# A second fold of the tokens ahead of a Fourier mixing step: fewer matmul columns for a longer chain of small operations

## The chip, the cores and the metric

One core of one Trainium2 chip. The metric is the device time of one execution in microseconds. The engines are named as the profile names them: PE is TensorE's matmuls, PEld its weight loads, DVE is VectorE, ACT is ScalarE, POOL is GpSimd. All data are fp32; each fp32 matmul shows in the trace as two records (the transform's 14 matmuls a batch as 28: 112 of `pz` and `pzt` in the four batches of the kernel before).

## The reference, cut to what matters

An mLSTM attention block produces `x` of 4 batches x 768 tokens x 320 features. Then comes a Fourier mixing and a two-layer MLP (1280 wide):

```python
def _moe_ref(x, w_ch1, w_ch2):
    X = np.fft.fft(x, axis=1)          # over the 768 tokens
    X = np.fft.fft(X, axis=2)          # over the 320 features
    u = x + np.real(X).astype(np.float32)
    ...                                # un = layer norm of u
    ch = np.maximum(un @ w_ch1, 0.0) @ w_ch2
    return (u + ch).astype(np.float32)
```

The transform over the tokens is a product with a table of cosines and sines, on TensorE.

## The kernel before: the parts that the change touches

The program is a schedule of small pieces (`at(slot, phase, piece, ...)`), interleaved so that the attention of batch n+1 and the MLP of batch n fill TensorE between the steps of the mixing. The code counts batches from 0, the text from 1, so `b == 0` is batch 1.

The mixing already uses one symmetry of the tokens, t with S - t: VectorE adds and subtracts paired row blocks (`eo`), then folds the 320 features in the same way into `fe`, so three row blocks of 128 tokens (`TG = 3`) are left instead of six.

```python
def mix_fold(b, p):
    ...
    for i, op in ((0, OP.add), (1, OP.subtract)):
        nc.vector.tensor_tensor(out=eo[:, i], in0=x[:, c], in1=x[:, m], op=op)
    ...
    ends(nc.vector, fe[:, p], 0, every)
    halves(nc.vector, fe[:, p, 1:HALF_D], 0, every, OP.add)
    halves(nc.vector, fe[:, p, PAD:PAD + HALF_D - 1], 1, every, OP.subtract)
    if p == TG - 1:
        nc.gpsimd.tensor_copy(out=fe_odd[:, 0:NC], in_=fe[:, p, 0:NC])
        ends(nc.gpsimd, fe_odd, 1, first)
        halves(nc.gpsimd, fe_odd[first, 1:HALF_D], 1, first, OP.add)

def mix_products(p, out, i, m):        # i = 0: cosine part, i = 1: sine part
    fm = slice(i * PAD + m.start, i * PAD + m.stop)
    kw = dict(stop=(p == 0), skip_group_check=True)
    if i == 0 and p == TG - 1:         # this block: even and odd frequencies apart
        nc.tensor.matmul(out[:, 0:NK:2], fe[:, p, fm], ds_sb[:, p, 0, 0:NE], start=True, **kw)
        nc.tensor.matmul(out[:, 1:NK:2], fe_odd[:, m], ds_sb[:, p, 0, NE:], start=False, **kw)
    else:                              # NK = 385 frequencies at once
        nc.tensor.matmul(out, fe[:, p, fm], ds_sb[:, p, i], start=(p == TG - 1), **kw)
```

`mix_seq` runs these products for features 0 to 127 (the two "big parts", cosine and sine, each into its own bank), `mix_tail` for the features left over: the cosine half of the tail writes partitions 0 to 63 of one bank, the sine half partitions 64 to 127 (a bank is a buffer into which TensorE writes results). For batches 2 to 4 the schedule gives each big part a slot of its own, with products of the MLP between:

```python
def plan_mix(b, s0, x_done, s_feat, s_add, s_turn):
    for j in range(TG):
        p = TG - 1 - j
        at(x_done[j], FILL + 0.5, mix_fold, b, p)
        if b == 0:
            ...
        else:
            at(s0, FILL_PE + 4, mix_seq, b, p, (0,))
            at(s0 + 1, FILL_PE + 4, mix_seq, b, p, (1,))
            at(s0 + 2, FILL_PE + 4, mix_tail, b, p)
```

In the MLP, VectorE's `add` (h = h + bank) frees the bank that a later product needs:

```python
    def add(h, bank):
        nc.vector.tensor_tensor(out=h, in0=h, in1=bank, op=OP.add)
```

## Time and profile before

| | before |
|---|---|
| time, first 3 runs | 446.88 us median (446.79 to 449.14) |
| profiled run: span, mean granted clock | 444.9 us, 0.996 |
| TensorE busy | 426.2 us, 96% |
| VectorE, ScalarE, GpSimd busy | 56%, 37%, 36% |
| the three changed transforms begin at | 142.91, 236.33 and 334.73 us |

TensorE, busy 96% of the span, is read here as the bound: a microsecond in which it stands still is counted as a microsecond lost. Two views that the prediction below uses in words only. The clock row of the page has one digit per fortieth of the span, 9 meaning 90% or more of full speed; the 8 is the half clock at the start-up (0.50 from 25.74 to 29.15 us):

```profile
PEclk9989999999999999999999999999999999999999
```

And TensorE's timeline at batch 2's tail (start, duration, operation, output<-inputs, count). Records of the cosine half (L627, L628) and of the sine half (L630) start together, at 156.28. The tail ends where the next group starts, at 158.37, so it takes 2.09 us:

```profile
156.28 0.35 PE L627 MATMUL pzt<-ds_sb,fe 128*64 128x193 f32 x1
156.28 0.54 PE L630 MATMUL pzt<-ds_sb,fe 128*64 128x385 f32 x1
...
156.95 1.49 PE L630 MATMUL pzt<-ds_sb,fe 128*64 128x385 f32 x8
158.37 1.88 PE L875 MATMUL po<-w_sb,hT 128*128 128x320 f32 x6
```

### The profile page before, as it was taken

Reading aid. Unit: us, or ns where it says so; the run is one execution under the profiler, and the core shown is the slowest. Engines: PE = TensorE matmul, PEld = TensorE weight load, DVE = VectorE, ACT = ScalarE, POOL = GpSimd, SP = SyncE. Lnnn points to the kernel's source line nnn. Section 1 sums busy time; section 2 is a strip of 40 time slices with the busy share of each in tenths; the row PEclk is TensorE's granted clock in tenths of the full one; section 3 lists DMA queues with packets and bytes.
Section 4 is the critical chain, followed back from the end, with each engine's and each line's share of the span. In section 5 each row is a group of like instructions: output and inputs, shape, how many; then the busy total and the mean of one; then the engine's idle time right before and its main releaser. Section 6 shows DMA issues by size and latency. Waiting matters only on the chain.

```text
span 444.9 us, 7313 instructions
## 1 busy us (share of the span) xinstructions
PE 426.2 (96%) x2680; PEld 285.4 (64%) x2680; DVE 250.5 (56%) x626; ACT 166.6 (37%) x442; POOL 159.0 (36%) x177
## 2 busy tenths in 40 slices
PE   8978989999899999989999999999999999999996
PEld 7767546666567777845556777775556677545774
DVE  8788784779986346587732266567630452343000
ACT  6957266584551223453243224443320031232000
POOL 5563101454333312045664303525661000477100
PEclk9989999999999999999999999999999999999999
DMA  7889944569364234157101432410000000000000
GB/s 238 257 237 338 285 129 134 184 195 288 110 177 138 76 123 137 55 156 219 40 1 49 139 119 97 125 31 1 2 0 15 16 26 18 16 0 1 31 29 29
DMA packets 20707, 47.37 MB, mean 106 GB/s; under 512 B 2816, under 2 KB 9344, under 8 KB 20544
## 3 DMA queue, kind: packets, MB, share of 16 engines
q1 hardware_dynamic: 20672, 46.91, 33.7%
q8 instruction: 21, 0.34, 0.3%
q14 instruction: 14, 0.11, 0.1%
HBM read 42.79 MB, written 4.11 MB: 105 GB/s over the span
## 4 chain that ended last, share of the span: by engine, by line
PE 75%; DVE 14%; issue 4%; ACT 3%; DMA 2%; POOL 2%; SPq 0%; DVEq 0%; POOLq 0%; ACTq 0%
PE po L875 29%; PE pm L822 13%; PE ps L455 4%; PE ph L476 4%; PE pm L827 4%; PE pu L661 4%; PE ph L469 3%; PE pz L630 3%; PE pm L760 3%; PE put L701 2%; PE pzt L630 2%; PE px L525 1%; DVE W L461 1%; DVE eo L588 1%; DMA G_d<-g 1%
## 5 line engine op out<-in xcount | busy, mean ns | idle before, releaser
L875 PE MATMUL po<-w_sb,hT 128*128 128x320 f32 x480 | 135.2, 434 | 0.0
L875 PEld LDWEIGHTS po<-w_sb,hT 128*128 128x128 f32 x480 | 89.7, 190 | 38.1 <-issue 2.0
L834 POOL TENSOR_SCALAR hT<-hT 128x384 f32<-128x384 f32 x45 | 66.2, 1492 | 86.2 <-DVE hT L831 86.2
L831 DVE TENSOR_TENSOR hT<-hT,pm 128x384 f32<-128x384 f32 x60 | 30.6, 549 | 38.2 <-ACT hT L853 25.7
L881 DVE SCALAR_TENSOR_TENSOR ot<-po,rstd,u 128x320 f32<-128x320 f32 x24 | 13.2, 548 | 69.0 <-PE po L875 69.0
L433 POOL TENSOR_SCALAR_AFFINE_SELECT W<-W 128x1024 f32<-128x1024 f32 x18 | 20.9, 1164 | 82.6 <-ACT W L411 78.6
L411 ACT ACTIVATE W<-W,colT 128x128 f32<-128x128 f32 x144 | 45.1, 395 | 0.0
L461 DVE TENSOR_TENSOR W<-ps,W 128x512 f32<-128x512 f32 x48 | 30.7, 680 | 10.7 <-POOL W L433 9.9
L822 PE MATMUL pm<-uT,w_sb 128*128 128x384 f32 x90 | 33.1, 496 | 1.6 <-DVE hT L831 0.9
L760 PE MATMUL pm<-uT,w_sb 128*128 128x384 f32 x80 | 29.6, 499 | 0.5 <-DVE u L683 0.4
L706 ACT COPY uT<-put 128x384 f32<-128x384 f32 x24 | 10.9, 480 | 49.6 <-PE put L701 49.6
L455 PE MATMUL ps<-qk 40*128 40x128 f32 x384 | 29.1, 290 | 0.2
L421 POOL TENSOR_TENSOR qg<-qk,Gb 128x512 f32<-128x512 f32 x19 | 26.4, 1388 | 4.9 <-DMA Gb<-G_d 4.8
L455 PEld LDWEIGHTS ps<-qk 40*128 40x128 f32 x384 | 24.5, 193 | 5.0 <-issue 1.0
L476 PE MATMUL ph<-W,kvt 128*41 128x128 f32 x384 | 26.2, 277 | 0.6 <-DVE W L461 0.6
L469 PEld LDWEIGHTS ph<-qg,C 128*128 128x128 f32 x160 | 20.8, 197 | 9.2 <-issue 3.2
L469 PE MATMUL ph<-qg,C 128*128 128x128 f32 x160 | 22.6, 286 | 3.9 <-POOL qg L421 2.4
L827 PE MATMUL pm<-uT,w1t_sb 64*128 64x384 f32 x120 | 25.2, 514 | 1.1 <-DVE hT L831 1.1
L822 PEld LDWEIGHTS pm<-uT,w_sb 128*128 128x128 f32 x90 | 16.1, 189 | 15.1 <-DVE hT L831 4.6
L476 PEld LDWEIGHTS ph<-W,kvt 128*41 128x41 f32 x384 | 19.7, 117 | 3.9 <-DVE W L461 1.0
L514 ACT COPY h<-ph 41x512 f32<-41x512 f32 (+1 forms) x16 | 9.3, 581 | 32.3 <-PE ph L476 32.2
L827 PEld LDWEIGHTS pm<-uT,w1t_sb 64*128 64x128 f32 x120 | 11.8, 185 | 12.3 <-issue 8.2
(164 smaller groups left out, 636.6 us busy)
## 6 DMA issues: line engine op xcount, KB each, us to landing
W<-M_d SPq DMA_DIRECT2D x18, 512.0 KB
kvt<-in_kv SPq DMA_DIRECT2D x24, 324.0 KB
qk<-in_qkT SPq DMA_DIRECT2D x48, 160.0 KB
raw<-in_w SPq DMA_DIRECT2D x10, 640.0 KB
Gb<-G_d SPq DMA_DIRECT2D x38, 128.0 KB
so<-in_o SPq DMA_DIRECT2D x24, 160.0 KB
out<-ot SPq DMA_DIRECT2D x24, 160.0 KB
ds_sb<-in_dft_s SPq DMA_DIRECT2D x1, 1155.0 KB
```

Of the source, the lines that this page charges most:

```text
L411: nc.scalar.activation(out=k.W[:, h, :], in_=M, func=AF.Exp, scale=-1.0, bias=colT[:, c, 0, b * H + h:b * H + h + 1])
L421: nc.gpsimd.tensor_tensor(out=k.qg, in0=k.qk[:, 0], in1=k.Gb, op=OP.mult)
L455: nc.tensor.matmul(k.ps[hip][:, p, :], k.qk[r, 1, p, :], k.qk[r, 0, p, :], start=True, stop=True)
L461: nc.vector.tensor_tensor(out=Wv, in0=k.ps[hip], in1=Wv, op=OP.mult)
L469: nc.tensor.matmul(k.ph[:, p, :], k.C[:, p, :], k.qg[:, p, :], start=(p == 0), stop=False, skip_group_check=True)
L476: nc.tensor.matmul(k.ph[hip * 64:hip * 64 + D1, p, :], k.v1[:, 2 * p + hip, :], k.W[:, 2 * p + hip, :], start=(c == 0 and p == 0), stop=Tr ...
L760: nc.tensor.matmul(k.pm[i], w1_sb[:, ch, f0:f0 + L], u[2 * ch], start=(ch == 0), stop=False)
L822: nc.tensor.matmul(bank, w, u, start=start, stop=True, skip_group_check=True)
L827: nc.tensor.matmul(bank, block(w1t_sb, i)[rows], mlp_u(gr, 1)[rows], start=False, stop=True, skip_group_check=True)
L831: nc.vector.tensor_tensor(out=h, in0=h, in1=bank, op=OP.add)
L834: nc.gpsimd.tensor_scalar(out=h, in0=h, scalar1=-1.0, scalar2=0.0, op0=OP.mult, op1=OP.max)
L875: nc.tensor.matmul(k.po, k.h[gr][f][:, i * L:(i + 1) * L], w2_sb[:, f, :], start=(f == 0), stop=(f == NFF - 1))
```

## The change

The intent: the 385 frequencies split into even and odd ones, and for each kind the table is symmetric or antisymmetric in t with S/2 - t. So blocks 0 (F) and 2 (F2) can be added and subtracted once more before the products. Each even or odd set then needs two row blocks in place of three: 3080 columns per batch instead of 4620, in the same number of matmuls (14). Table and output are then read and written with a stride of two. Batch 1 stays as it was. The core of the diff:

```diff
+    def mix_fold_again(b):
+        k = mixes.setdefault(b, Mix())
+        F, G, F2 = (fe[:, p] for p in range(TG))
+        k.less = eo_p.tile(...)  # cut
+        cos = (slice(0, 1), slice(0, NC))
+        nc.gpsimd.memset(F2[0:1, PAD:], 0.0)
+        nc.vector.tensor_tensor(out=k.less, in0=F, in1=F2, op=OP.subtract)           # L617
+        nc.gpsimd.tensor_copy(out=k.less[cos], in_=fe_odd[cos])                      # L618
+        nc.gpsimd.tensor_copy(out=fe_odd[:, 0:NC], in_=G[:, 0:NC])                   # L619
+        nc.gpsimd.tensor_tensor(out=fe_odd[cos], in0=G[cos], in1=F[cos], op=OP.subtract)  # L620
+        nc.gpsimd.tensor_tensor(out=G[cos], in0=G[cos], in1=F[cos], op=OP.add)       # L621
+        nc.vector.tensor_tensor(out=F, in0=F, in1=F2, op=OP.add)                     # L622
+        nc.gpsimd.tensor_copy(out=F[cos], in_=F2[cos])                               # L623
...
+    def mix_products_again(k, p, out, i, m):
+        ...  # F, G, less: the feature slices of the blocks
+        every, even, odd = slice(0, NK), slice(0, NK, 2), slice(1, NK, 2)
+        if i == 0:
+            products = ((even, F, 0), (even, G, 1), (odd, less, 0), (odd, fe_odd[:, m], 1))
+        else:
+            products = ((even, less, 0), (odd, F, 0), (every, G, 1))
+        for n, (cols, f, p) in enumerate(products):
+            nc.tensor.matmul(out[:, cols], f, ds_sb[:, p, i, cols], start=(n == 0), stop=(n == len(products) - 1),
+                             skip_group_check=True)
...
-            else:
+            elif j == 0:
+                at(x_done[-1], FILL + 0.55, mix_fold_again, b)
                 at(s0, FILL_PE + 4, mix_seq, b, p, (0,))
                 at(s0 + 1, FILL_PE + 4, mix_seq, b, p, (1,))
                 at(s0 + 2, FILL_PE + 4, mix_tail, b, p)
...
+    at(24, FILL + 0.4, lambda: nc.gpsimd.memset(ds_sb[0:1, 0, 0, :], 1.0))
```

The L numbers are the lines under which the changed kernel's profile shows them; its matmuls of the transform are L651, its MLP products L854 and L859, its MLP add L863. The one-row operations (`cos`) mend the first row of each block, whose tokens have no ordinary partner.

More of the change, by code (lines that the diff above doesn't have):

```diff
@@ L601, in mix_fold @@
         if p == TG - 1:
-            nc.gpsimd.tensor_copy(out=fe_odd[:, 0:NC], in_=fe[:, p, 0:NC])
+            if b == 0:
+                nc.gpsimd.tensor_copy(out=fe_odd[:, 0:NC], in_=fe[:, p, 0:NC])
             ends(nc.gpsimd, fe_odd, 1, first)
             halves(nc.gpsimd, fe_odd[first, 1:HALF_D], 1, first, OP.add)
+    def mix_fold_again(b):
+        k = mixes.setdefault(b, Mix())
+        F, G, F2 = (fe[:, p] for p in range(TG))
+        k.less = eo_p.tile([L, 2, DM], FP, name="eo", tag="eo").rearrange("p two n -> p (two n)")[:, 0:2 * PAD]
+        cos = (slice(0, 1), slice(0, NC))
[7 more added lines that the diff above has]
+        nc.gpsimd.tensor_copy(out=F[cos], in_=F2[cos])
     def mix_seq(b, p, parts):
@@ L612, in mix_seq @@
         for i in parts:
-            mix_products(p, k.pz[i], i, slice(0, L))
+            (mix_products if b == 0 else mix_products_again)(k, p, k.pz[i], i, slice(0, L))
     def mix_tail(b, p):
@@ L620, in mix_tail, with mix_products @@
         for i in range(2):
-            mix_products(p, k.pzt[i * 64:(i + 1) * 64], i, slice(L, PAD))
-    def mix_products(p, out, i, m):
+            (mix_products if b == 0 else mix_products_again)(k, p, k.pzt[i * 64:(i + 1) * 64], i, slice(L, PAD))
+    def mix_products_again(k, p, out, i, m):
+        fm = slice(i * PAD + m.start, i * PAD + m.stop)
+        F, G, less = fe[:, 0, fm], fe[:, 1, fm], k.less[:, fm]
+        every, even, odd = slice(0, NK), slice(0, NK, 2), slice(1, NK, 2)
[6 more added lines that the diff above has]
+                             skip_group_check=True)
+    def mix_products(k, p, out, i, m):
         fm = slice(i * PAD + m.start, i * PAD + m.stop)
```

## The prediction

> **What bounds the kernel now.** I read the busy table of the page first, then the slices and clock, then the chain of work that ended last, then the TensorE waits after 140 us, and last the timelines around each place where a batch's tokens are folded.
>
> ```profile
> span 444.9 us, 7313 instructions
> PE 426.2 (96%) x2680; PEld 285.4 (64%) x2680; DVE 250.5 (56%) x626; ACT 166.6 (37%) x442; POOL 159.0 (36%) x177
> ...
> PE 75%; DVE 14%; issue 4%; ACT 3%; DMA 2%; POOL 2%; SPq 0%; DVEq 0%; POOLq 0%; ACTq 0%
> ```
>
> TensorE is busy 96% of the span and carries 75% of the chain. So a microsecond of matmul saved is a microsecond saved, and a microsecond in which TensorE is made to wait is one lost. The waits of TensorE from 140 us to the end, where all three changed folds lie, add up to only 3.4 us:
>
> ```profile
> PE pm L827 <- DVE hT L831: 1.1, 1, 1.1
> PE pm L822 <- DVE hT L831: 0.9, 4, 0.3
> PE pm L822 <- DVE uT L810: 0.6, 1, 0.6
> PE pz L630 <- DVE fe L595: 0.5, 1, 0.5
> PE pm L822 <- DVE ot L881: 0.3, 1, 0.3
> ```
>
> Two places matter. Batch 2 has no slack between fold and transform: its transform starts at 142.91 and then waits for VectorE's last fold (timeline, TensorE and VectorE):
>
> ```profile
> 143.56 0.81 PE L630 MATMUL pz<-ds_sb,fe 128*128 128x385 f32 x2
> 144.91 0.91 PE L630 MATMUL pz<-ds_sb,fe 128*128 128x385 f32 x2 [0.54 <-DVE fe L595]
> ...
> 143.39 1.24 DVE L591 COPY fe<-eo 128x2 f32<-128x2 f32 x1
> 144.55 0.81 DVE L595 TENSOR_TENSOR fe<-eo 128x159 f32<-128x159 f32 x2
> ```
>
> Batches 3 and 4 fold at 216 and 315 us and transform at 236 and 335 us, 20 us later. But right after the fold VectorE's queue holds adds that free banks for the running MLP, and the chain runs through VectorE there:
>
> ```profile
> 215.64 0.55 DVE L595 TENSOR_TENSOR fe<-eo 128x159 f32<-128x159 f32 x2
> 216.10 0.54 DVE L831 TENSOR_TENSOR hT<-hT,pm 128x384 f32<-128x384 f32 x1
> ...
> 218.86 1.47 DVE L831 TENSOR_TENSOR hT<-hT,pm 128x384 f32<-128x384 f32 x3
> ```
>
> The second tail product of the MLP (started 216.84) needs the add that ended at 216.64: 0.2 us of slack. The next block, at 219.46, already waited 0.22 us.
>
> [...] after the idle around 22 to 25.5 us the granted clock was 0.50 from 25.7 to 29.1 us. That window still held 0.86 us of matmuls in 3.41[...]. [...] the two tail halves write partitions 0-63 and 64-127: both start at once, and the tail takes 2.1 us, not the 3.9 us of its records in series. [...] the stride-2 outputs of the first row block (193 columns) ran 0.163 us a record, just their columns, so I take no penalty. [...]
>
> **The change part by part.** Removed, for batches 2 to 4: matmul columns. Every fp32 matmul shows as two records; a record of 385 columns takes 0.323 us (six in 1.94), one of 193 takes 0.163. Before, the cosine and the sine part each took 1155 columns, 1.94 us. Now they are four times 193 (8 x 0.163 = 1.30) and 193+192+385 (1.30). The number of matmuls and weight loads stays 14; loads don't bind, because 128-column records elsewhere (eight in 0.89 us) sustain 0.11 us. Two big parts save 0.64 us each. The tail, if its halves still overlap, goes from 2.09 to about 1.44, saving 0.65. That is 1.94 us a batch, 5.8 us in all.
>
> Added: a chain that hops between VectorE and GpSimd. In order: subtract of 128x384 on VectorE, 0.56 (the 128x384 subtracts of the MLP's sums: 0.557); GpSimd copy 1x161, 0.35, and copy 128x161, 0.35 (348 ns, same instruction as the removed one); two GpSimd tensor-tensors of 1x161, 0.51 each (512 ns for 1x159); add of 128x384 on VectorE, 0.56, which must wait for the two because they read the row it overwrites; then a GpSimd copy 1x161, 0.35. Each hand-over costs 0.06 to 0.07 us, as between GpSimd's dependent casts. VectorE is held from its first to its last of these: 0.62 + 0.41 + 0.42 + 0.58 + 0.58 + 0.63 = 3.2 us. To the last copy it is 3.65 us. The 192-element memset (0.26 us, estimated from 120 ns for 31 and 525 ns for 512 elements) precedes it and is hidden. One memset of a table row at slot 24 is off the path.
>
> Where it lies. Batch 2: all products now need the complete second fold; the built order puts the first behind the last GpSimd copy. The ordinary fold should end about 145.2 [...], so TensorE restarts at about 148.9 and stands still for 6.0 us from 142.9. The group of output products that began at 145.82 begins at 148.9 + 1.3 = 150.2: 4.4 us late. The sine part gives back 0.64 and the tail 0.65: net 3.1 us lost. [...] Batch 2: +4.4.
>
> Batches 3 and 4: the built order has the subtract and the waiting add ahead of the MLP's add, so that add starts at 219.3 instead of 216.1, and everything of VectorE behind it (13 small operations, three adds) moves too. TensorE stops about 3.2 us less slack in each batch, roughly 3.1 to 3.2; later 1.94 come back: +1.25 each. The stop is about 2.4 us of true idleness[...]. Together +2.9.
>
> Sum: 446.9 + 4.4 + 2.9 = 454.2; I say 454.0, since a stop lets the other engines catch up and may swallow some of the 2 us that TensorE waits for VectorE at 190 to 197 us.
>
> **The rivals.** (a) The matmuls decide: if TensorE were not stopped, because the second fold hid in the 20 us of slack, the result would be 446.9 - 5.8 = 441. For it: 96% busy, and the real slack in batches 3 and 4. Against it: batch 2 has none, and the slack is of the transform, not of VectorE's queue[...]. (b) The halves of the tail don't overlap any more: program order now has four products (eight records) of one half before the other's first, where it had two; then the tail takes 2.6 us and the result is 3.4 us worse, 457.5. [...] I give it 20%. (c) The clock never halves: 452.5. Against it: the drop at 25.7 us. (d) Stride-2 reads of the table or more weight switches make a 193-column record as long as a 385-column one: all 5.8 us vanish, about 460. The table's old half was contiguous, so no line excludes it; I give it 7%.
>
> **Range and chances.** From 450.0 (no halved clock and part of the stops swallowed elsewhere) to 457.5 (serial tail or both clock drops). Slower by over 2% means above 455.8: 0.25. Faster by over 2%, below 437.9, would need more than the whole saving: 0.02. Within 2%: 0.73.
>
> **What would show it.** TensorE busy time falls in the transform: pz from 1.94 to 1.30 us a part, tail near 1.4. In batch 2 a TensorE wait near 6 us for GpSimd's last copy, with the clock at half shortly after. In batches 3 and 4, VectorE's add waits about 2 us for GpSimd, and a TensorE tail product waits 2.4 to 3 us for VectorE. Wrong if the waits of TensorE after 140 us stay near 3.4 us, if the records of 193 columns last over 0.2 us apiece, or if the chain passes through GpSimd's ReLUs instead.

How the sum came about: it was 446.9 + 4.4 + 2.9 = 454.2 us, given as 454.0. The 4.4 of batch 2 are the 3.1 above and 1.25 for a lower clock after the stop; the 2.9 are 1.25 and 0.2 for a lower clock in each of batches 3 and 4. These three terms, 1.65 us in all, were the estimate, and what they rested on was not shown by the trace before, which has one stretch of half clock in its span (25.74 to 29.15 us, after the window of 22.33 to 25.74 with 0.86 us of matmuls). The 145.2 us for the end of the ordinary fold and the 20% for rival (b) stand as estimates.

## The result, and the profile after

| | before | after |
|---|---|---|
| time, median of 6 runs | 448.09 us (446.79 to 450.89) | 463.88 us (462.70 to 465.35) |
| ratio of fast runs | | 1.0348 [1.0310, 1.0386] |
| profiled run: span, mean clock | 444.9 us, 0.996 | 463.6 us, 0.966 |

The ratios here and below are the mean time of one kernel's fast runs over that of the other's in the same rounds, so not quite the ratio of the medians. The change is slower by 3.5%, against 1.6% predicted; 463.88 lies above the range.

The page of the changed kernel, the same lines as shown of before:

```profile
span 463.6 us, 7339 instructions
PE 435.5 (94%) x2680; PEld 294.0 (63%) x2680; DVE 253.6 (55%) x632; ACT 166.6 (36%) x442; POOL 165.1 (36%) x193
...
PEclk9979999999999799997979999999989999999999
...
PE 80%; DVE 11%; ACT 3%; issue 2%; DMA 2%; POOL 2%; SPq 0%; DVEq 0%; POOLq 0%; ACTq 0%
```

TensorE has a third fewer transform columns in three batches and yet was busy 9.3 us longer. The clock row points to why: four further digits are below 9. A matmul at half clock counts as busy for about twice as long: the first four records of the transform took 1.45 us in batch 2 (150.83 to 152.28, clock 0.50) and 0.69 us in batch 3 (253.02 to 253.71, clock 1.00). The chain ends up in TensorE more than before (80% for 75%), not less.

The waits of TensorE from 100 us on (longest last):

```profile
PE pz L651 <- POOL fe L623: 5.6, 1, 5.6
PE pm L859 <- DVE hT L863: 5.4, 3, 2.2
```

The first is the one stop of batch 2; of the second line's three waits two are the new stops of batches 3 and 4, and the third, 1.1 us, was there before. Batch 2 in TensorE's timeline:

```profile
150.83 1.66 PE L651 MATMUL pz<-ds_sb,fe 128*128 128x193 f32 x4 [5.58 <-POOL fe L623]
152.28 0.85 PE L651 MATMUL pz<-ds_sb,eo 128*128 128x192 f32 x2
152.92 0.85 PE L651 MATMUL pz<-ds_sb,fe_odd 128*128 128x192 f32 x2
153.56 2.74 PE L907 MATMUL po<-w_sb,hT 128*128 128x320 f32 x6
```

From 150.83 to 153.56 are 2.73 us for eight records that the prediction put at 1.30. Batch 3, where the fold itself is needed only at 253.02, but VectorE's queue is held by it (first fence VectorE, second TensorE):

```profile
227.19 0.56 DVE L617 TENSOR_TENSOR eo<-fe 128x384 f32<-128x384 f32 x1
229.73 0.56 DVE L622 TENSOR_TENSOR fe<-fe 128x384 f32<-128x384 f32 x1 [1.98 <-POOL fe L621]
230.21 0.55 DVE L863 TENSOR_TENSOR hT<-hT,pm 128x384 f32<-128x384 f32 x1
```

```profile
230.81 2.93 PE L859 MATMUL pm<-uT,w1t_sb 64*128 64x384 f32 x6 [2.15 <-DVE hT L863]
```

VectorE waits 1.98 us for GpSimd's L621 in the middle of the fold, the MLP's add (L863) stands behind it, and TensorE waits 2.15 us for that add. Batch 4 has the same wait, 2.15 us at 335.22.

Now the clock. The windows view gives per stretch (us from the start) the busy time of PE, PEld, DVE, ACT and POOL with counts, then the mean granted clock of TensorE, the DMA share and GB/s. In this trace half clock begins at 25.79, 148.66, 206.69, 230.58 and 336.40 us, each time for 6.83 or 3.41 us, and at 462.69, to the end; all the changes lie whole multiples of 3.413 us apart. The stretches are cut there, to a tenth, and are called windows below. First batch 2's stop, then batch 3's, then batch 4's, each with what followed:

```profile
145.30:148.70 3.40, 0.00 (x0) 0.00 (x0) 2.47 (x5) 0.00 (x0) 2.27 (x4) 0.99 0.11 40
148.70:152.10 3.40, 1.27 (x4) 1.27 (x5) 2.22 (x4) 0.00 (x0) 2.51 (x6) 0.50 0.19 65
152.10:155.50 3.40, 3.40 (x10) 2.81 (x9) 1.13 (x2) 1.70 (x6) 0.45 (x1) 0.50 0.25 73
227.20:230.60 3.40, 1.46 (x4) 0.29 (x3) 1.42 (x3) 0.48 (x1) 1.90 (x5) 1.00 0.00 0
230.60:234.00 3.40, 3.19 (x7) 1.51 (x8) 3.06 (x17) 0.00 (x0) 0.46 (x2) 0.50 0.02 5
234.00:237.40 3.40, 3.40 (x6) 1.85 (x6) 0.44 (x1) 0.97 (x2) 3.40 (x3) 0.50 0.00 0
333.00:336.40 3.40, 1.25 (x7) 0.68 (x6) 2.09 (x10) 0.00 (x0) 1.34 (x3) 1.00 0.02 5
336.40:339.80 3.40, 3.40 (x7) 1.59 (x6) 2.29 (x9) 0.49 (x1) 1.78 (x2) 0.50 0.00 0
```

Each stop left TensorE busy for 0.00, 1.46 and 1.25 us of a 3.40 us window, and each time the next windows ran at 0.50: two after batches 2 and 3, one after batch 4. So a stop of 2.15 us was followed by half clock both times; e4 below tests whether it is the cause. One more episode, from 206.69 to 213.52 us, follows no stop of the change, but the window ahead of it holds the wait of 1.1 us that was there before (it ends at 205.07):

```profile
203.30:206.70 3.40, 2.30 (x11) 1.14 (x11) 3.19 (x10) 1.52 (x5) 0.00 (x0) 1.00 0.82 259
206.70:210.10 3.40, 3.40 (x28) 2.90 (x28) 0.34 (x1) 0.00 (x0) 2.89 (x3) 0.50 0.84 241
```

Last the tail of batch 2:

```profile
164.52 0.87 PE L651 MATMUL pzt<-ds_sb,fe 128*64 128x193 f32 x4
165.24 0.56 PE L651 MATMUL pzt<-ds_sb,eo 128*64 128x192 f32 x4
...
166.72 1.61 PE L907 MATMUL po<-w_sb,hT 128*128 128x320 f32 x5
```

It takes 166.72 - 164.52 = 2.20 us, for a third fewer columns than the 2.09 us before. The first four records, two products of the cosine half, run alone for 0.72 us. Only then do records of both halves (the L651 line with eo x4) run side by side.

Where the 18.8 us between the two profiled runs lie, by the times at which TensorE passed the same point of the program (the last column is the delay that arose since the row above):

| TensorE reaches | before | after | shift of the stage |
|---|---|---|---|
| output products ahead of batch 2's transform | 140.11 | 142.29 | +2.18 |
| end of batch 2's tail | 158.37 | 166.72 | +6.17 |
| last MLP product ahead of batch 3's stop | 215.99 | 226.90 | +2.56 |
| transform of batch 3 | 236.33 | 253.02 | +5.78 |
| end of batch 3's tail | 250.08 | 265.71 | -1.06 |
| the same ahead of batch 4's stop | 315.68 | 331.32 | +0.01 |
| transform of batch 4 | 334.73 | 354.58 | +4.21 |
| end of batch 4's tail | 346.19 | 364.99 | -1.05 |
| end | 444.85 | 463.65 | 0.00 |

The first row is ahead of all changed work: the start-up's half clock lasted two windows (25.79 to 32.61) and not one (25.74 to 29.15), and a wait of TensorE behind loaded data was longer (3.15 us in place of 2.41). The start-up's half clock differs from run to run: the third digit of the page's clock row is 8 before and in e2, 7 in the change, e1 and e4, and 5 in e3. I take these 2.2 us for the run's chance; that is argued, not shown. The rest is divided with two experiments that keep the clock up (e4_warm and e10_warm_tail below): in e4 the second stage costs 3.99 us, and in both the stops of batches 3 and 4 cost 3.20 us each. So of 6.17, 5.78 and 4.21 the clock has about 2.2, 2.6 and 1.0, and the third row is all clock: 2.6. Together: clock about 8.3 us (5.8 after the stops of the change), stops less saved matmuls 18.8 - 8.3 - 2.2 = 8.3 us, start-up 2.2 us.

### The profile page after: what moved, and what is told of

It reads as the page before. It is cut to its first block, busy times and chain, and to the rows that moved or that the text cites. A ratio compares the mean times of both kernels' runs of the same rounds, so it can differ in the third digit from the quotient of the medians.

```text
span 463.6 us, 7339 instructions
## 1 busy us (share of the span) xinstructions
PE 435.5 (94%) x2680; PEld 294.0 (63%) x2680; DVE 253.6 (55%) x632; ACT 166.6 (36%) x442; POOL 165.1 (36%) x193
## 4 chain that ended last, share of the span: by engine, by line
PE 80%; DVE 11%; ACT 3%; issue 2%; DMA 2%; POOL 2%; SPq 0%; DVEq 0%; POOLq 0%; ACTq 0%
PE po L907 28%; PE pm L854 13%; PE pm L859 5%; PE ps L455 5%; PE pm L792 5%; PE ph L476 5%; PE ph L469 4%; PE pu L692 3%; PE pz L651 2%; PE put L732 2%; PE px L525 2%; PE pm L796 1%; PE pzt L651 1%; DVE eo L588 1%; DMA G_d<-g 1%
## 5 line engine op out<-in xcount | busy, mean ns | idle before, releaser
L863 DVE TENSOR_TENSOR hT<-hT,pm 128x384 f32<-128x384 f32 x60 | 30.7, 550 | 41.9 <-ACT hT L885 29.3
L854 PE MATMUL pm<-uT,w_sb 128*128 128x384 f32 x90 | 34.5, 516 | 0.9 <-DVE uT L842 0.6
L859 PE MATMUL pm<-uT,w1t_sb 64*128 64x384 f32 x120 | 29.3, 550 | 5.4 <-DVE hT L863 5.4
L455 PE MATMUL ps<-qk 40*128 40x128 f32 x384 | 30.1, 297 | 0.2
L792 PE MATMUL pm<-uT,w_sb 128*128 128x384 f32 x80 | 29.6, 499 | 0.5 <-DVE u L714 0.4
L476 PE MATMUL ph<-W,kvt 128*41 128x128 f32 x384 | 27.9, 289 | 0.6 <-DVE W L461 0.6
L421 POOL TENSOR_TENSOR qg<-qk,Gb 128x512 f32<-128x512 f32 x19 | 26.6, 1399 | 4.6 <-DMA Gb<-G_d 4.6
L854 PEld LDWEIGHTS pm<-uT,w_sb 128*128 128x128 f32 x90 | 17.6, 203 | 14.9 <-DVE hT L863 2.8
L859 PEld LDWEIGHTS pm<-uT,w1t_sb 64*128 64x128 f32 x120 | 12.9, 196 | 18.4 <-issue 8.8
L476 PEld LDWEIGHTS ph<-W,kvt 128*41 128x41 f32 x384 | 20.9, 123 | 4.2 <-DVE W L461 1.0
```

The lines of the kernel that those rows point to most:

```text
L421: nc.gpsimd.tensor_tensor(out=k.qg, in0=k.qk[:, 0], in1=k.Gb, op=OP.mult)
L455: nc.tensor.matmul(k.ps[hip][:, p, :], k.qk[r, 1, p, :], k.qk[r, 0, p, :], start=True, stop=True)
L476: nc.tensor.matmul(k.ph[hip * 64:hip * 64 + D1, p, :], k.v1[:, 2 * p + hip, :], k.W[:, 2 * p + hip, :], start=(c == 0 and p == 0), stop=Tr ...
L792: nc.tensor.matmul(k.pm[i], w1_sb[:, ch, f0:f0 + L], u[2 * ch], start=(ch == 0), stop=False)
L854: nc.tensor.matmul(bank, w, u, start=start, stop=True, skip_group_check=True)
L859: nc.tensor.matmul(bank, block(w1t_sb, i)[rows], mlp_u(gr, 1)[rows], start=False, stop=True, skip_group_check=True)
```

## The experiments

The theory: the loss beyond the prediction is the clock, which three stops bring to half, each for one or two windows, and the tail, which does not shrink. A first rival: the stops alone, with the hand-overs between VectorE and GpSimd in them, make the whole loss, and the clock is a side effect. A second: the new products themselves (strided table reads and outputs) are slow. The runs were made in three groups; the kernel before ran beside each, at 449.81 us (7 runs), 449.08 us (11) and 449.42 us (11) median. e1 and e2 give a wrong result, and so does e5; all others were correct. Diffs are against the changed kernel.

**e1_products_only.** The products of the change without the second fold (wrong result): what do the products alone do?

```diff
     def mix_fold_again(b):
         k = mixes.setdefault(b, Mix())
-        k.less = eo_p.tile(...)
-        ...                      # all eight operations of the second fold
+        F, G, F2 = (fe[:, p] for p in range(TG))
+        k.less = F2
...
-        F, G, less = fe[:, 0, fm], fe[:, 1, fm], k.less[:, fm]
+        F, G, less = fe[:, 2, fm], fe[:, 1, fm], fe[:, 2, fm]
```

> The new products without the second fold; the result is wrong on purpose, since the products read fold buffers that don't wait for the last fold. Theory (the matmul term of the prediction was right, the loss is all in stops and clock): TensorE's transform parts of batches 2 to 4 shrink from 1.94 to 1.30 us, the tail from 2.1 to 1.4, no new stop, so 448 - 5.8 - 0.5 = 441.5 us, ratio 0.986. Rival (the new products are themselves slow: stride-2 reads, more weight switches, a serial tail): no gain or a loss, 448 to 452 us, ratio 1.00 to 1.01.

Measured: 445.52 us, ratio 0.9897 [0.9844, 0.9949]. The products are faster than before, though by less than 2%, so the second rival falls: no part of the loss is theirs. But the tail took 2.19 us without any fold:

```profile
157.70 1.27 PE L643 MATMUL pzt<-ds_sb,fe 128*64 128x193 f32 x8
158.74 0.33 PE L643 MATMUL pzt<-ds_sb,fe_odd 128*64 128x192 f32 x1
...
159.89 1.34 PE L899 MATMUL po<-w_sb,hT 128*128 128x320 f32 x4
```

The tail's share of the saving is missing whatever the fold does.

**e2_batch2_only** and **e3_batches34_only.** The change in batch 2 alone (its one-row table memset corrupts the other batches, so the result is wrong), and in batches 3 and 4 alone (correct; the memset moved behind batch 2).

```diff
-            (mix_products if b == 0 else mix_products_again)(k, p, k.pz[i], i, slice(0, L))
+            (mix_products_again if b in (1,) else mix_products)(k, p, k.pz[i], i, slice(0, L))   # e3: (2, 3)
...                               # the same condition for the tail, the fold and the plan
+            elif b not in (1,):
+                at(s0, FILL_PE + 4, mix_seq, b, p, (0,))
+                ...
```

> Second fold and new products for batch 2 alone, the old ones for batches 3 and 4 (their result is wrong on purpose: the table row that the new products need is already changed). Theory: a stop of 5.6 us before the transform of batch 2, then one or two clock windows at 0.5: stop 5.0 net, clock about 2.5 to 3.5, matmuls -1.9, so +6 us, ratio 1.013. Rival (the loss is spread evenly over the three batches): +5.2 us, ratio 1.0117; rival (the slow clock is set off later, by something else): a stop of 5.6 us and clock 1.0 until 190 us, ratio 1.007.

> Second fold and new products for batches 3 and 4 alone, batch 2 as before; right result. Theory: two stops of about 2.2 us, each followed by a half clock for 3.4 or 6.8 us: each batch +3.1 (stop and lost overlap) + 1.7 to 3.4 (clock) - 1.9 = +2.9 to 4.6, together +6 to +9 us, ratio 1.013 to 1.02. Without any fall of the clock it would be +2.5 us, ratio 1.006. No half clock near 207 us is expected if that one was an echo of batch 2; if it also shows here, it has another cause.

Measured: 454.53 us, 1.0121 [1.0065, 1.0177], and 457.53 us, 1.0174 [1.0127, 1.0222]. Both losses are real and add up to 2.95% of the 3.48%. In e2's profile (mean clock 0.988) the clock was half from 146.93 to 153.76, right after the stop of 5.6 us; in e3's (0.977) from 222.67 to 229.50 and from 328.49 to 331.90, after the two stops of 2.2 us, and the wait line is that of the change:

```profile
PE pm L863 <- DVE hT L867: 5.4, 3, 2.2
```

Neither has the episode near 207 us. In e2 the window before that place was as empty as the changed kernel's, and the clock stayed at 1.00 (same columns as above):

```profile
201.54:204.95 3.41, 2.31 (x12) 1.26 (x10) 3.24 (x9) 1.27 (x5) 0.00 (x0) 1.00 0.81 259
204.95:208.36 3.41, 3.41 (x54) 2.66 (x54) 0.80 (x4) 1.01 (x3) 3.16 (x3) 1.00 0.88 225
```

**e4_warm.** The stops stay, but matmuls whose result nobody reads fill them, so that TensorE never rests for long (correct result): what is the clock's share?

```diff
+        if b == 1 and parts == (0,):
+            for _ in range(11):
+                nc.tensor.matmul(k.pz[0][:, 0:2 * L], rest[:, 0:L], rest, start=True, stop=True, skip_group_check=True)
...
+    for s in (73, 105):
+        at(s, MAIN - 0.5, idle_products, 5)
```

> The changed kernel with matmuls of zeros in the three stops (11 of 256 columns ahead of the transform of batch 2, 5 of 256 columns in the MLP block of batch 1 and of batch 2 where VectorE holds TensorE up). They take 4.7 and 2.2 us of time that TensorE stood idle, so they cost nothing if the stop is the stop. Theory (half of the loss is the clock): clock stays at 1.00 from 40 us on, time = 448 + stops 5.0 + 2 x 3.1 - matmuls 5.8 = 453.5 us, ratio 1.012, against 1.035 of the change. Rival (the half clock is a consequence of something else, or costs little): ratio stays above 1.03.

Measured: 456.81 us, 1.0161 [1.0109, 1.0213], in place of 1.0348. Added matmuls made the kernel faster by 1.8%, and the first rival falls: about half of the loss is not the stops but what they do to the clock. The three stops left no half clock, and the records of the transform have their full-speed length again (the 7 near the middle of the clock row is the episode near 207 us):

```profile
PEclk9979999999999999997999999999999999999999
...
144.65 4.91 PE L633 MATMUL pz<-rest 128*128 128x256 f32 x22
150.43 0.95 PE L654 MATMUL pz<-ds_sb,fe 128*128 128x193 f32 x4 [0.87 <-POOL fe L623]
151.22 0.50 PE L654 MATMUL pz<-ds_sb,eo 128*128 128x192 f32 x2
151.56 0.51 PE L654 MATMUL pz<-ds_sb,fe_odd 128*128 128x192 f32 x2
151.90 2.31 PE L910 MATMUL po<-w_sb,hT 128*128 128x320 f32 x8
```

From 150.43 to 151.90: 1.47 us in place of 2.73; the changed kernel's own batch 3, away from any stop, has 1.37 (253.02 to 254.39). The profiled run still had half clock at 203.67 to 210.50, so that episode doesn't need one in batch 2.

**e5_tail_alternating.** e1 with the tail's products issued in turn, one of each half (wrong result like e1): does the order decide whether the halves overlap?

```diff
-        for i in range(2):
-            (mix_products if b == 0 else mix_products_again)(k, p, k.pzt[i * 64:(i + 1) * 64], i, slice(L, PAD))
+        if b == 0:
+            ...                    # as before
+        else:
+            parts = [mix_products_again(..., i, slice(L, PAD), one=True) for i in range(2)]   # a list of products
+            for n in range(4):
+                for i in range(2):
+                    if n < len(parts[i]):
+                        parts[i][n]()
```

> The products-only kernel (wrong on purpose) with the tail's seven products issued in turn from the two halves, not four and then three. Theory (the halves overlap only where the other half's product is near in the queue): the tail falls from 2.19 to about 1.45 us in each of batches 2 to 4, 2.2 us in all, ratio 0.985 against 0.990. Rival (193-column tail products don't overlap at all, the order is not it): 2.2 us still, ratio 0.990.

Measured: 444.03 us, 0.9867 [0.9824, 0.9910]; the interval overlaps e1's, so the times alone don't part them. The trace does: the tail took 157.55 - 156.03 = 1.52 us, in place of 2.19.

```profile
156.03 1.54 PE L650 MATMUL pzt<-ds_sb,fe 128*64 128x193 f32 x12
...
157.55 1.88 PE L911 MATMUL po<-w_sb,hT 128*128 128x320 f32 x6
```

**e6_fold_on_vector.** The small operations and the memset of the second fold move from GpSimd to VectorE, at the same places, so that no hand-over is left (correct).

```diff
-        nc.gpsimd.tensor_copy(out=k.less[cos], in_=fe_odd[cos])
+        nc.vector.tensor_copy(out=k.less[cos], in_=fe_odd[cos])
...                               # likewise the memset, both tensor_tensors and the two other copies
```

> The changed kernel with the five small operations and the memset of the second fold on VectorE in place of GpSimd, at the same places. Theory (it is VectorE's time at that place that stops TensorE; the hand-overs only lengthen it): VectorE's part takes 0.56 + 0.56 and five or six operations of 0.17 to 0.32, about 2.4 to 2.7 us in place of 3.2, so the stops shrink by 0.5 to 0.8 us in batches 3 and 4 and from 5.6 to about 4.5 in batch 2; the clock still halves: 460 us, ratio 1.025 against 1.035. Rival (the hand-overs to GpSimd are the whole loss): stops near zero, ratio 1.00 or less.

Measured: 462.85 us, 1.0304 [1.0261, 1.0346]. The stops of batches 3 and 4 fell from 2.15 to 1.8 us, but batch 2's stayed at 5.6 us where I had expected less. The waits, and VectorE's timeline in batch 2, where a copy ran slowly (0.65 us; 0.23 in batch 3) and a memset now stands in the queue that before had been hidden:

```profile
PE pz L651 <- DVE fe L623: 5.6, 1, 5.6
PE pm L859 <- DVE hT L863: 4.8, 3, 1.8
...
146.63 0.22 DVE L616 MEMSET fe<- 1x192 f32 x1
146.88 0.56 DVE L617 TENSOR_TENSOR eo<-fe 128x384 f32<-128x384 f32 x1
147.48 0.65 DVE L618 COPY eo<-fe_odd 1x161 f32<-1x161 f32 x1
```

The profiled run's mean clock was 0.966, as the change's. So the hand-overs are a small part of the loss. What counts more, by these traces, is that VectorE's queue is held by a fold for some 3 us at a bad moment; the next three runs test that.

**e7_late34.** If the moment is what counts, the fold of batches 3 and 4 can move into their 20 us of slack. Batches 3 and 4 alone, fold on VectorE, behind the MLP's adds, tail in turn (correct):

```diff
-                at(x_done[-1], FILL + 0.55, mix_fold_again, b)
+                at(s0 - 5, FILL_PE + 0.2, mix_fold_again, b)
...                               # plus e3's conditions, e5's tail, e6's engine
```

> Batches 3 and 4 alone by the second fold, all of it on VectorE and moved five slots ahead of the transform, behind the MLP's adds, where VectorE idles about 3 us; tail in turn; batch 2 as before; right result. Theory (placement, not the operations, costs): no new stop and no half clock in either batch, 448 - 2 x 1.9 = 444 us, ratio 0.991. Rival (any place holds the MLP up[...]): 1.00 or more.

Measured: 445.98 us, 0.9893 [0.9848, 0.9937]. No new stop in the trace. Two of its six runs, the profiled one among them, counted as slow (clock 0.985; the profile had half clock from 201.18 to 208.01); the ratio is of the four fast ones.

**e8_late_all** and **e9_late_all_2.** The same for all three batches. Batch 2 has no slack, so its big parts move two slots back, beside its tail. In e8 the second fold stays right behind the first; in e9 it goes one slot later, behind VectorE's weighings of the attention scores (both correct).

```diff
-                at(x_done[-1], FILL + 0.55, mix_fold_again, b)
-                at(s0, FILL_PE + 4, mix_seq, b, p, (0,))
-                at(s0 + 1, FILL_PE + 4, mix_seq, b, p, (1,))
+                at(*((x_done[-1], FILL + 0.55) if b == 1 else (s0 - 5, FILL_PE + 0.2)), mix_fold_again, b)  # e8
+                at(*((x_done[-1] + 1, FILL + 0.9) if b == 1 else (s0 - 5, FILL_PE + 0.2)), mix_fold_again, b)  # e9
+                at(s0 + 2 * (b == 1), FILL_PE + 4, mix_seq, b, p, (0,))
+                at(s0 + 1 + (b == 1), FILL_PE + 4, mix_seq, b, p, (1,))
...                               # plus e5's tail, e6's engine
```

> As the kernel before with the second fold in all three batches: on VectorE, late in batches 3 and 4, tail in turn, and the two big transform parts of batch 2 moved two slots back, beside its tail, so that they don't wait for the fold; right result. Theory: no stop, 448 - 3 x 1.9 - 0.5 = 441.7 us, ratio 0.986. Rival (in batch 2 four banks are then held at once, or the copies of the three parts come too late, and TensorE waits 1 to 2 us there): 443.5 us, ratio 0.99; with a half clock on top 446, ratio 0.995.

> The previous all-late kernel with the second fold of batch 2 behind VectorE's two weighings of the attention block instead of ahead of them (there TensorE waited 2.3 us for them, and the clock halved for 6.8 us). Theory (the only fault was again a place ahead of work that TensorE needs): no stop at batch 2, 449 - 3 x 1.9 - 0.5 = 443 us, ratio 0.986 to 0.988. Rival (holding three banks at once, or moving the two parts back, costs by itself): a wait of TensorE of 1 us or more for a bank near 150 to 165 us, ratio 0.993 or more.

e8 missed: 448.12 us, 0.9967 [0.9930, 1.0004]. The stop had moved to the scores, which waited 2.31 us for the weighing that now stood behind the fold, and then the clock was half for 6.8 us: sixteen records of the scores took 2.67 us (below) in place of 1.16 in e9. The fold itself had also stretched, from 2.9 us (e6, batch 3) to 5.1 us (148.29 to 153.37): three of its small operations took 0.66, 1.02 and 1.28 us in place of 0.23, 0.25 and 0.32; what slowed them is not shown.

TensorE's line:

```profile
154.61 2.67 PE L455 MATMUL ps<-qk 40*128 40x128 f32 x16 [2.31 <-DVE W L461]
```

e9 hit: **442.78 us (440.94 to 444.05), 0.9867 [0.9817, 0.9916]** against the kernel before, so faster than both kernels, though against the kernel before by less than 2%. What is left of batch 2's stop is a quarter of a microsecond, and between the start-up and the end the clock was never half (mean 0.992, as in e1):

```profile
154.13 0.95 PE L658 MATMUL pz<-ds_sb,fe 128*128 128x193 f32 x4 [0.24 <-DVE fe L623]
```

**e10_warm_tail.** e4 and e5's tail order together (correct): do clock and tail account for the whole excess?

```diff
+        if b == 1 and parts == (0,):      # e4's matmuls
+            ...
+            parts = [mix_products_again(..., one=True) for i in range(2)]   # e5's tail
```

> The changed kernel with both disputed terms put right: matmuls of zeros in the three stops and the tail in turn. Theory (the prediction's sum without its clock term and with the tail it counted on was right: 5.0 + 2 x 3.1 - 5.8 = +5.4 us): ratio 1.012, below the 1.016 of the zeros alone; three stops filled, no half clock after them. Rival (a further loss is hidden): 1.016 or more.

Measured: 456.87 us, 1.0166 [1.0092, 1.0240]: not the gain over e4 that I expected, and inconclusive, since the interval holds both. In the trace the tail of batch 2 did take 1.50 us (163.28 to 164.78), but the profiled run's mean clock was 0.985, and its four runs had 0.985 to 0.992. The kernel before varies in the same way beside it: 444.92 us at clock 1.000, 449.42 at 0.992, 451.24 at 0.984. A gain of 2 us is below what such rounds can part.

## Why the prediction was wrong

Right:

- **What bounds, and where the stops are.** TensorE stood still where the prediction said, for the reasons it gave. Batch 2: 6.0 us predicted, 5.58 measured, for GpSimd's last copy. (One reading in that sum is off by 0.16 us: the output products, put at 145.82, began at 145.66.) Batches 3 and 4: about 2.4 us predicted, 2.15 measured, for the MLP's add behind the fold.
- **The length of the fold.** VectorE held for 3.2 us by the working, 3.1 us measured (227.19 to 230.29); its add waited 1.98 us for GpSimd, "about 2" predicted. At full clock each of these stops cost 3.20 us (3.15 predicted).
- **The big parts.** Eight records at 1.37 us at full clock (1.30 predicted, 1.94 before), so 0.171 us a record with a stride of two in table and output; rival (d) is wrong, as e1 shows.
- **VectorE slower beside GpSimd** was reckoned with. In the kernel before, VectorE's copy L591 of batch 2 took 1.24 us (143.39 to 144.63) while GpSimd's L421 ran (143.10 to 144.60), in the change 1.22 us beside the same operation; the median of its twelve is 0.16. The two adds behind it (L595) took 0.81 us before, beside GpSimd's L445, and 0.54 in the change, where GpSimd had a memset of 0.27 us. More than this is not shown.
- **The direction.** A loss was predicted; the chance of over 2% was put at 0.25 and the range ended at 457.5.

Wrong, by the terms of the sum:

- **The clock term, 1.25 + 0.2 + 0.2 us, is the step that failed.** It measured about 2.2 + 2.6 + 1.0 after the stops: 5.8 in place of 1.65. (Another 2.6 near 207 us follows a wait that the kernel before has too.) Two things were off in it. Half clock after the 2.4 us stops was weighted down by chance, at 0.2 us each; both stops were followed by it, in the change and in e3, in the change after windows that were 43 and 37% busy. That these would suffice could not be read from the trace before: it has one fall, after a window 25% busy, and windows of 59 and 55% (shown below) with full clock after them. And the half clock lasted longer: after batch 2's stop TensorE worked 4.7 us at 0.50 (150.83 to 155.49), for which the estimate had 1.25 us of loss, and after batch 3's 6.83 us, for which it had 0.2. e4 measured it apart: the same stops, filled with matmuls, cost 1.6% and not 3.5%.
- **The tail, 2.09 to 1.44 us, measured 2.20.** Rival (b), given 20%, was half right: the halves still overlapped, but only in the last two products of the one and the first two of the other. With four products of one half ahead of the other's first in program order, the second half's first record came 0.72 us late, when four of the eight records ahead of it had run. In turn (e5, e9, e10) the same products took 1.50 to 1.54. Against the 1.44 predicted that is 0.76 us a batch, 2.3 us in all, and makes up most of the difference between the net 5.6 us of stops and matmuls that the prediction had and the 8.3 us found.
- **Start-up, 2.2 us in the profiled pair**, was no term, and the change doesn't touch it.

Rival (c), that the clock never halves, is what e4 built by hand, but for the episode near 207 us.

What stays open. Why an episode lasts one window or two: the second window followed windows that were 37%, 93% and 100% busy, and batch 4's single one followed one of 100%. And which partly idle windows are followed by half clock: the share of busy time alone doesn't say. The kernel before had windows of 59% and 55% with no half clock after them:

```profile
42.80:46.21 3.41, 2.00 (x16) 1.56 (x18) 3.26 (x10) 1.11 (x4) 1.25 (x4) 1.00 1.02 350
114.48:117.89 3.41, 1.88 (x14) 1.20 (x14) 3.10 (x11) 2.61 (x9) 0.68 (x1) 1.00 0.05 11
```

Near 207 us the clock fell in the changed kernel and in e4, each time after a window that was 68% busy; in e2 it stayed at 1.00 after a window as busy (2.31 of 3.41 us). In the kernel before, where the old wait of 1.1 us ends at 196.72, the cut at 196.40 parts it, the two windows are 77 and 91% busy, and the clock stayed. So the share of busy time that is followed by half clock is not found here, and that the change makes this episode more likely is not shown. Without it the ratio would still be near 1.03.

## What to carry to other kernels

On an engine that is 96% busy, price a stop by what was seen to follow it too: here waits that the profile shows as 2.15 us cost 3.2 us each and up to 2.6 us more at half clock, and useless matmuls in the gap made the kernel 1.8% faster. When a fold or any preparation is added, ask not when its result is needed but what stands behind it on its engine (here the MLP's add, behind a fold that waited 1.98 us, and TensorE waited 2.15 us for the add): the second fold cost 3.5% in one place and, some slots later, on VectorE alone and with a better issue order, went with a gain of 1.3% (e9). Here products into the two halves of a bank, partitions 0 to 63 and 64 to 127, overlapped better when the program order had them near each other (a tail of 1.52 us in e5 in place of 2.19 in e1), so try issuing such products in turn.
